# A decode layer on one Trainium2 core: keys, wo and w1 in one transfer each, keys transposed in place, one exp per row

## The chip, the cores and the metric

The kernel runs on one core of one Trainium2 chip. The metric is the device time of one execution in microseconds (us). Before the change it is 139.44 us, the median of three runs (139.34 to 139.45).

The core has five engines with a queue each, which work on their own and wait for each other through semaphores: TensorE (PE; its weight loads are listed as PEld), VectorE (DVE), ScalarE (ACT), GpSimd (POOL) and SyncE (SP), which here only issues transfers. Sixteen DMA engines carry data between the chip's main memory and the on-chip memory of 128 partitions. Matmuls write their sums to PSUM, and another engine has to copy them from there.

## The reference

A transformer layer for one new token in each of four sequences (B = 4, model width D = 1024), in bf16. Everything is read once from main memory; the weights and the cache are nearly all of the data.

```python
def _A_ref(x, k_cache, v_cache, wq, wo):       # 32 query heads, 4 key heads, head width 128
    W = min(4096, max(256, Sk // 4))           # Sk = 8192, so the last W = 2048 positions
    q = (x @ wq).reshape(B, 1, 32, 128).transpose(0, 2, 1, 3)
    k = repeat(k_cache[:, :, Sk - W:, :], 8, axis=1)
    v = repeat(v_cache[:, :, Sk - W:, :], 8, axis=1)
    p = softmax(einsum("bhqd,bhkd->bhqk", q, k) * 128 ** -0.5)
    o = einsum("bhqk,bhkd->bhqd", p, v)
    return o.transpose(0, 2, 1, 3).reshape(B, 1, 4096) @ wo

def _B_ref(x, w1, w3, w2):                     # inner width 3584
    return (silu(x @ w1) * (x @ w3)) @ w2

h  = x + _A_ref(_layernorm(x), k_cache, v_cache, wq, wo)
h2 = h + _B_ref(_layernorm(h), w1, w3, w2)
```

Sizes in bf16: wq 8.4 MB, keys 8.4 MB, values 8.4 MB, wo 8.4 MB, w1, w3 and w2 7.3 MB each.

## The kernel before, in words

**Memory.** All large inputs pass through five slots of 32 KB per partition. `ring` (L106) is the list of what goes through them, in order: the first half of wq (four of its eight rows per partition), the keys of two batches, those of the other two, two slots for transposed keys (which no transfer fills), the second half of wq, the values in two slots, wo in two, w1 in two, w3 in two, w2 in two. `fill` (L118) allocates the next slot and issues its transfers on SP (L132); it goes on until the slot that it wants is the one that was taken five places earlier and is not yet marked as used. `done` (L139) marks a part as used and calls `fill`. The instruction itself waits for the semaphores of the last readers. So each transfer may run up to five slots ahead of its use. Keys, values and wo go as four transfers each of 16 KB per partition, wq as two of 32 KB, w1 and w3 as two of 28 KB each, w2 as six of 14 to 2 KB. SP takes its instructions strictly in order. x itself is small: four transfers of 2 KB on ScalarE's queue (L149).

**Order of the work.** The schedule is written out by hand: each engine takes its instructions in the order of the program.

1. x is loaded, transposed on VectorE (L225) and normalised (`layernorm_T`, L192), with sums over partitions by a matmul (L198).
2. `query(0)` (L237): the first half of x @ wq, 32 matmuls of 512 columns, four at a time on four groups of 32 array columns.
3. Keys (L258 to L270): for each batch and each eight blocks of 128x128, eight transposes on TensorE into PSUM (L264), and one eviction of 1024 columns into a slot of the ring, in turn by VectorE (L266) and ScalarE (L268).
4. `query(1)`, then q is copied (L274, L275), transposed (L278) and spread into `Qm` (L284).
5. Attention, batch by batch and staggered by the loop at L395: `scores` (L295, 16 matmuls of 512 columns per batch, L299), `row_max` (L310), `softmax` (L325), `transpose_p` (L349), `output` (L358). The scores of 8 positions by 4 key heads share a row. `softmax` takes the exponential four times for each batch, once for each key head, with a bias that makes the entries of the other key heads zero (L336 to L339). `transpose_p` turns 32x32 squares on VectorE (L351). `output` sums the row totals by a matmul (L360), multiplies with the values (L374), scales and masks (L383) and folds four parts into one (L391).
6. Attention's output is gathered by eight matmuls (L414), cast, transposed and copied into `oP` (L422 to L427). Then wo: 128 matmuls of 256 columns, four at a time (L439). x is added (L449).
7. The second layer norm, then w1 (gate, L463), exp, plus one, reciprocal (L477 to L481), w3 (up, L463), the product (L485), a transpose (L225), and w2 (L496), which is used in the six pieces in which it comes. The sum with h goes out in four transfers (L510).

## Time and profile before

One execution was profiled. Its own time is 139.33 us and its span, from the first to the last instruction, 137.5 us (137.54 in the trace).

| | before |
|---|---|
| time of the three runs, median | 139.44 us |
| time of the profiled execution | 139.33 us |
| its span | 137.5 us |
| data read | 55.58 MB, 404 GB/s over the span |
| TensorE busy | 78.7 us (57%) |
| VectorE busy | 52.6 us (38%) |
| ScalarE busy | 42.7 us (31%) |
| mean granted clock of TensorE | 0.812 |

How to read it. The page divides the span into 40 slices of 3.44 us, and gives for each engine how much of a slice it was busy, in tenths. The DMA row does this for the mean of the 16 DMA engines. The list of queues says which queue's packets took which share of 16 engines' span; q1 is SP's. The chain of work that ended last is followed back from the end of the program: at each step to what the instruction had waited for. The groups give, for instructions of one line and kind, how often they ran, their total and mean duration, and how long their engine had been idle just before them and for whom. Windows give the busy time of an engine in chosen stretches, with the granted clock of TensorE (1.00 or 0.50 in this trace). The trace also has the records of single instructions, DMA packets and the changes of the clock. A busy share is a mean over stages: the stage tells what a microsecond is worth.

### The profile page before, as it was taken

What the parts mean: (1) busy time and instruction counts of PE and PEld (TensorE: products, weight loads), DVE (VectorE), ACT (ScalarE), POOL (GpSimd) and SP (SyncE); (2) the same over time, 40 slices, a digit from 0 to 9 for tenths busy, and PEclk for the clock granted to TensorE, in tenths of its full rate; (3) what the DMA queues carried; (4) which work ended last, traced back from release to release, by engine and by line L of the source; (5) the groups of instructions that cost most, each with busy time, mean ns of one, the idle gap of its engine ahead of it and who ended that gap; (6) DMA issues with size and microseconds to landing.
All of it is one profiled execution on the core that took longest, in us unless ns stands there. A gap on an engine that the chain in (4) does not pass through costs nothing.

```text
span 137.5 us, 2022 instructions
## 1 busy us (share of the span) xinstructions
PE 78.7 (57%) x866; PEld 45.4 (33%) x868; DVE 52.6 (38%) x97; ACT 42.7 (31%) x57; POOL 4.2 (3%) x18
## 2 busy tenths in 40 slices
PE   0000299999903889328936997948539600834271
PEld 0000139898801422114303353536424300322240
DVE  3001505666700235187165359551330596160001
ACT  1200006989820325998803940000040200000000
POOL 7400000000000000000000000000000000000000
PEclk9999999999995599955595599995995995595555
DMA  5998999999899999999999999999999999999950
GB/s 152 458 459 382 429 434 434 415 438 505 376 410 429 415 438 419 434 429 415 443 417 429 422 467 425 438 417 434 425 430 425 425 447 388 414 437 431 400 219 2
DMA packets 3529, 55.72 MB, mean 405 GB/s; under 512 B 416, under 2 KB 448, under 8 KB 704
## 3 DMA queue, kind: packets, MB, share of 16 engines
q1 hardware_dynamic: 3472, 55.58, 95.2%
q8 instruction: 7, 0.11, 0.3%
q10 hardware_dynamic: 48, 0.01, 0.0%
q14 instruction: 2, 0.02, 0.0%
HBM read 55.58 MB, written 0.01 MB: 404 GB/s over the span
## 4 chain that ended last, share of the span: by engine, by line
DMA 51%; PE 28%; DVE 13%; ACT 4%; issue 2%; SPq 1%; DVEq 0%
DMA s_wq<-in_A_wq_dram 31%; DMA s_w<-in_B_w_dram 20%; PE o_ps L374 11%; ACT P L339 4%; PE y_ps L439 4%; PE sc_ps L299 3%; DVE PT L351 3%; PE q_ps L244 2%; DVE om L391 2%; PE gu_ps L463 2%; DVE od L383 2%; PE tot_ps L360 1%; PE nm_ps L328 1%; PE on_ps L414 1%; SPq L132 1%
## 5 line engine op out<-in xcount | busy, mean ns | idle before, releaser
L339 ACT ACTIVATE P<-sc_ps,bias 128x512 bf16<-128x512 f32 x16 | 19.7, 1421 | 10.8 <-DVE bias L336 10.8
L374 PE MATMUL o_ps<-s_v,PT 128*128 128x512 bf16 x62 | 18.4, 457 | 0.3 <-issue 0.2
L268 ACT COPY s_kT<-kt_ps 128x1024 bf16<-128x1024 bf16 x16 | 15.6, 1012 | 6.8 <-PE kt_ps L264 6.8
L264 PE MATMUL kt_ps<-ident,s_k 128*128 128x128 bf16 x256 | 16.1, 219 | 1.1 <-ACT s_kT L268 1.0
L264 PEld LDWEIGHTS <-s_k 128*128 128x128 bf16 x256 | 15.0, 98 | 2.9 <-issue 2.5
L463 PE MATMUL gu_ps<-s_w,n_T 128*32 128x448 bf16 x128 | 9.8, 474 | 9.8 <-DMA s_w<-in_B_w_dram 8.0
L266 DVE COPY s_kT<-kt_ps 128x1024 bf16<-128x1024 bf16 x16 | 11.1, 692 | 10.1 <-PE kt_ps L264 10.1
L244 PE MATMUL q_ps<-s_wq,n_T 128*32 128x512 bf16 x64 | 7.2, 630 | 7.4 <-DMA s_wq<-in_A_wq_dram 5.6
L496 PE MATMUL y_ps<-s_w,hg_T 128*32 128x256 bf16 x112 | 6.6, 386 | 7.9 <-DMA s_w<-in_B_w_dram 5.3
L374 PEld LDWEIGHTS <-PT 128*128 128x128 bf16 x64 | 7.6, 123 | 9.8 <-issue 5.5
L208 ACT ACTIVATE rstd<-rstd,eps_t 128x4 f32<-128x4 f32 x2 | 0.6, 297 | 32.4 <-DVE rstd L207 32.4
L198 PE MATMUL sums_ps<-both,ones_f 128*128 128x64 f32 x4 | 1.1, 374 | 16.1 <-DVE both L196 16.1
L351 DVE STREAM_TRANSPOSE PT<-P 128x2048 bf16<-128x2048 bf16 x4 | 9.2, 2304 | 2.7 <-ACT P L339 2.7
L463 PEld LDWEIGHTS <-n_T 128*32 128x32 bf16 x128 | 4.4, 122 | 14.5 <-issue 11.5
L299 PE MATMUL sc_ps<-s_kT,Qm 128*32 128x512 bf16 x64 | 8.5, 603 | 0.4 <-DVE Qm L284 0.4
L496 PEld LDWEIGHTS <-hg_T 128*32 128x32 bf16 x112 | 4.2, 124 | 10.8 <-issue 6.8
L383 DVE SCALAR_TENSOR_TENSOR od<-o_ps,rinv,jmask 128x512 f32<-128x512 f32 x4 | 3.0, 750 | 9.4 <-PE o_ps L374 9.3
L198 PEld LDWEIGHTS sums_ps<-both,ones_f 128*128 128x128 f32 x4 | 0.8, 250 | 16.4 <-DVE both L196 16.4
L315 PE MATMUL mx_ps<-ident_f,rmax 128*1 128x128 f32 x8 | 1.9, 333 | 7.4 <-DVE rmax L313 7.4
L244 PEld LDWEIGHTS <-n_T 128*32 128x32 bf16 x64 | 2.4, 139 | 10.8 <-issue 8.6
L479 DVE RECIPROCAL eg<-eg 128x896 f32<-128x896 f32 x1 | 5.8, 5753 | 0.0
L439 PE MATMUL y_ps<-s_wo,oP 128*32 128x256 bf16 x128 | 4.9, 326 | 1.5 <-DVE oP L427 1.5
(68 smaller groups left out, 59.7 us busy)
## 6 DMA issues: line engine op xcount, KB each, us to landing
s_w<-in_B_w_dram SPq DMA_DIRECT2D x4, 3584.0 KB
s_wq<-in_A_wq_dram SPq DMA_DIRECT2D x2, 4096.0 KB, 12.3
s_k<-in_A_k_cache_dram SPq DMA_DIRECT2D x4, 2048.0 KB, 20.5
s_v<-in_A_v_cache_dram SPq DMA_DIRECT2D x4, 2048.0 KB
s_wo<-in_A_wo_dram SPq DMA_DIRECT2D x4, 2048.0 KB, 25.1
s_w<-in_B_w_dram SPq DMA_DIRECT2D x1, 2048.0 KB, 24.7
s_w<-in_B_w_dram SPq DMA_DIRECT2D x1, 1792.0 KB
s_w<-in_B_w_dram SPq DMA_DIRECT2D x1, 1536.0 KB
```

What stands on the lines that cost most here:

```text
L244: nc.tensor.matmul(q_ps[hf][R * c : R * c + R], lhsT=xn_T[:, kc, :], rhs=w[:, kk, o : o + HALF * Dh], start=(kc == 0), stop=(kc == KC - 1) ...
L264: nc.tensor.transpose(out=kt_ps[:, jj], in_=k[:, jb * JB + jj, :], identity=ident[:])
L266: nc.vector.tensor_copy(out=kT[:, jb * JB : (jb + 1) * JB], in_=kt_ps[:])
L268: nc.scalar.copy(out=kT[:, jb * JB : (jb + 1) * JB], in_=kt_ps[:])
L299: nc.tensor.matmul(sc_ps[b][R * q : R * q + R], lhsT=Qm[:, b, g * R : (g + 1) * R], rhs=v[:, g, q], start=(g == 0), stop=(g == Hkv - 1), t ...
L339: nc.scalar.activation(out=P4[:, :, :, g], in_=sc_ps[b][:].rearrange("p (j i) -> p j i", i=L5), func=ACT.Exp, bias=bias[:, g : g + 1], sca ...
L351: nc.vector.transpose(out=PT[:].rearrange("p j h -> p (j h)"), in_=stage.pop(("P4", b))[:].rearrange("p j i g -> p (j i g)"),)
L374: nc.tensor.matmul(o_ps[:], lhsT=PT[:, i * JM : (i + 1) * JM, :].rearrange("p j h -> p (j h)"), rhs=v[:, i * JM : (i + 1) * JM, :], start= ...
L439: nc.tensor.matmul(y_ps[R * c : R * c + R, :], lhsT=oP[:, g, t, :], rhs=w[:, 0, o : o + DQ], start=(g == 0 and t == 0), stop=(g == Hkv - 1 ...
L463: nc.tensor.matmul(out_ps[hf][R * c : R * c + R], lhsT=hn_T[:, kc, :], rhs=w[:, kk, o : o + FH], start=(kc == 0), stop=(kc == KC - 1), til ...
L479: nc.vector.reciprocal(out=eg[:], in_=eg[:])
L496: nc.tensor.matmul(y2_ps[R * c : R * c + R, :], lhsT=hg_T[:, fc, :], rhs=w[:, ff, c * DQ : (c + 1) * DQ], start=(fc == 0), stop=(fc == FC ...
```

## The change

- **Memory.** The five slots become one tile, `ring`, of five units of 32 KB per partition, in which every input has a place written out by hand: wq in units 0 and 1, keys in 3 and 4, values 0 and 1 in 2, values 2 and 3 in 0, wo in 3 and 4, w1 in 1 and 2, w3 in 3 and 4, w2's first piece in 0 and its others in 1. Each transfer waits for the last readers and writers of the bytes that it overwrites, and of no others.
- **Transfers.** The first transfer is one of wq's eight rows (8 KB per partition), the second all keys (64 KB per partition), the third the other seven rows of wq (56 KB). wo goes in one transfer of 64 KB per partition and w1 in one of 56 KB. Values stay at 16 KB per transfer and w3 at 28 KB; w2 goes in pieces of 26, 16, 8, 4 and 2 KB. In all 16 large transfers stand where 24 stood. The transfers are issued from where they stand in the program: values 2 and 3 after half of the query, wo after the last scores, w1 after the matmuls of `output(1)`, w3 and the first piece of w2 after wo's matmuls, the rest of w2 after the gate's.
- **Keys.** A partition now holds 256 positions of one batch and key head. The transposes run in 16 steps of 16 blocks; the evictions write back over the blocks that were read, one of three on VectorE, two on ScalarE. All of them come ahead of the whole query. `scores` reads the transposed keys as pairs of neighbouring elements, 256 bytes apart, instead of single elements 8 bytes apart.
- **Softmax.** The maximum is taken for two batches at once. One exponential per batch goes over the row; VectorE then spreads each value over four columns, times a 0/1 mask of the key head (`spread`), and transposes.
- **After it.** The fold of `output` is two additions on POOL. Attention's output is gathered by four matmuls straight into the layout of `oP`. wo's matmuls are 64 of 512 columns, two at a time, and x is added by four matmuls into the same sum.
- **Layer norm and silu.** The copy and the square run on ScalarE, three small operations on POOL; the plus one of silu runs on ScalarE. Most constants are set up on POOL.

The diff, cut to its core:

```diff
-    wo_v = A_wo.rearrange("(g p t) n -> p g (t n)", g=Hkv, t=T)
+    KI = P // (B * Hkv)
+    KP = W // KI
+    KQ = KI // C
+    k_v = A_k_cache[:, :, Sk - W : Sk, :].rearrange("b g (i j) d -> (b g) i (j d)", j=KP)
+    v_v = A_v_cache[:, :, Sk - W : Sk, :].rearrange("b g (i j) d -> b i g (j d)", j=JR)
+    wo_v = A_wo.rearrange("(p t) n -> p (t n)", t=T)
...
+    ring = stream.tile([P, 5 * UNIT], BF16)
...
+    wq_s = at(0, KC, NQ)
+    k_s = at(3, KP, Dh)
+    v_s = [at((2, 0)[b // 2], 2, JR, Dh)[:, b % 2] for b in range(B)]
+    wo_s = at(3, T, D)
+    w1_s = at(1, KC, F)
+    w3_s = at(3, KC, F)
+    W2B = [13, 8, 4, 2, 1]
...
+    load(wq_s[:, :1, :], wq_v[:, :1, :])
+    load(k_s.rearrange("p j d -> p (j d)"), k_v)
+    load(wq_s[:, 1:, :], wq_v[:, 1:, :])
+    load_values(0)
+    load_values(1)
...
     def layernorm_T(h_T, tag):
-        nc.vector.tensor_copy(out=both[:, 0], in_=h_T[:, :, :B])
-        nc.vector.tensor_tensor(out=both[:, 1], in0=both[:, 0], in1=both[:, 0], op=ALU.mult)
+        nc.scalar.copy(out=both[:, 0], in_=h_T[:, :, :B])
+        nc.scalar.activation(out=both[:, 1], in_=h_T[:, :, :B], func=ACT.Square)
...
+    for n in range(KP // JB):
+        blocks = k_s[:, n * JB : (n + 1) * JB, :]
+        kt_ps = ps.tile([P, JB, P], BF16, tag=("scA", "ktA", "scB")[n % 3])
+        for jj in range(JB):
+            nc.tensor.transpose(out=kt_ps[:, jj], in_=blocks[:, jj, :], identity=ident[:])
+        if n % 3 == 0:
+            nc.vector.tensor_copy(out=blocks, in_=kt_ps[:])
+        else:
+            nc.scalar.copy(out=blocks, in_=kt_ps[:])
...
+    q_ps = ps.tile([P, 2, REP // 2, Dh], FP32, tag="scA")
+    for kc in range(KC):
...
+        if kc == KC // 2 - 1:
+            load_values(2)
+            load_values(3)
...
+    kT = k_s.rearrange("p (u v) (y q l) -> p y q u v l", v=JR, q=C, l=KQ)
...
     def scores(b, gs):
-        v = get("kT", b).rearrange("p j (q i g) -> p g q j i", q=C, g=Hkv)
...
-                    rhs=v[:, g, q],
+                    rhs=kT[:, Hkv * b + g, q],
...
+    def softmax(b):
+        p1 = act.tile([P, W // C], BF16, tag=("hg", "eg")[b % 2], name="p1")
+        nc.scalar.activation(
+            out=p1[:].rearrange("p (v l u) -> p u v l", l=KQ, u=L5 // KQ),
+            in_=sc_ps[b // 2][:, b % 2].rearrange("p (u v l) -> p u v l", l=KQ, v=JR),
+            func=ACT.Exp,
...
+    def spread(b):
+        P4 = ktpool.tile([P, JR * L5, Hkv], BF16, tag="P4")
+        nc.vector.tensor_tensor(
+            out=P4[:],
+            in0=stage.pop(("p1", b))[:].rearrange("p (x o) -> p x o", o=1).to_broadcast([P, JR * L5, Hkv]),
+            in1=gmask[:].to_broadcast([P, JR * L5, Hkv]),
+            op=ALU.mult,
+        )
...
+        o2 = act.tile([P, 2, Dh], FP32, tag="o2", bufs=1)
+        nc.gpsimd.tensor_tensor(out=o2[:], in0=od[:, :2], in1=od[:, 2:], op=ALU.add)
+        nc.gpsimd.tensor_tensor(out=om[:, b], in0=o2[:, 0], in1=o2[:, 1], op=ALU.add)
...
+    scores(0, (0, 1, 2, 3))
+    scores(1, (0, 1, 2, 3))
+    row_max(0)
+    scores(2, (0, 1))
+    bias_of(0)
+    softmax(0)
+    softmax(1)
+    scores(2, (2, 3))
+    scores(3, (0, 1, 2, 3))
+    load(wo_s, wo_v.rearrange("p (t n) -> p t n", t=T))
+    row_max(1)
+    spread(0)
+    bias_of(1)
+    softmax(2)
+    transpose_p(0)
+    spread(1)
+    softmax(3)
+    transpose_p(1)
+    total(0)
+    output(0)
+    spread(2)
+    transpose_p(2)
+    output(1)
+    load(w1_s, w1_v)
+    spread(3)
+    transpose_p(3)
+    total(1)
+    output(2)
+    output(3)
...
+    nc.scalar.copy(out=oP[:, :, :B], in_=on_ps[:].rearrange("p b t -> p t b"))
...
+    for t in range(T):
+        row = wo_s[:, t].rearrange("p (k i n) -> p i k n", k=2, i=2)
+        for i in range(2):
+            nc.tensor.matmul(
+                y_ps[R * i : R * i + R],
+                lhsT=oP[:, t, :],
+                rhs=row[:, i],
...
+    for i in range(2):
+        load(w3_s[:, 4 * i : 4 * i + 4, :], w3_v[:, 4 * i : 4 * i + 4, :])
+    load(w2_s[0], w2_v[:, : W2B[0], :])
...
+    up_projection(w1_s, gate_ps)
+    fc = W2B[0]
+    for w, n in zip(w2_s[1:], W2B[1:]):
+        load(w, w2_v[:, fc : fc + n, :])
+        fc += n
+    nc.scalar.activation(out=eg[:], in_=gate_ps[:, :, :FH], func=ACT.Exp, scale=-1.0)
+    nc.scalar.activation(out=eg[:], in_=eg[:], func=ACT.Identity, bias=1.0)
...
```

`load` issues one transfer on SP, `load_values(b)` the values of batch b, and `at(unit, ...)` is a view of `ring` from a unit on.

## The prediction

> **What bounds the kernel now.** I read three views in this order: the slices and queues of the page, the chain of work that ended last, and the windows of TensorE. The page first:
>
> ```profile
> DMA  5998999999899999999999999999999999999950
> ...
> q1 hardware_dynamic: 3472, 55.58, 95.2%
> ```
>
> The DMA row is at 8 or 9 tenths from the second slice to the thirty-eighth of 40, and SP's queue q1 alone fills 95.2% of the span of all 16 engines. In the trace's DMA packet records the first packet starts at 1.77 us, the last ends at 133.58 us, and in every stretch of 2 us from 2 to 132 the 16 engines are busy for all of it. The chain of waits says the same; columns are start, length, what:
>
> ```profile
> 13.65 29.70 DMA s_wq<-in_A_wq_dram
> ...
> 105.80 27.58 DMA s_w<-in_B_w_dram
> ```
>
> Both are transfers in a queue that never ran dry, and what the chain puts between them (attention, L299 to L427) did not stop the queue. So the kernel costs 55.58 MB at full rate, 1.77 us ahead of it and 3.96 us (137.54 - 133.58) behind it. The profiled execution took 139.33 us, 1.79 more than its span; the three runs have a median of 139.44. There are two ways to change the time: fewer engine-nanoseconds per byte, or a hole in the stream.
>
> **What the larger transfers remove.** Median packet durations in the records: 2 KB 84 ns, 4 KB 159, 8 KB 311, 12 KB 464, 14 KB 538, 16 KB 612, 28 KB 1066, 32 KB 1214. From 16 to 32 KB that is 602 ns per 16 KB and 10 ns fixed. So I estimate 56 KB at 2117 ns, 64 KB at 2418 (at most 2 x 1214 = 2428), 26 KB at 988. Each transfer has 128 packets, 8 per engine. Before, per engine: wq 16 x 1214, K, V and wo 96 x 612, w1 and w3 32 x 1066, w2 8 x (538+464+612+311+159+84), together 129.6 us. After: wq 8 x (311+2117), K 8 x 2418, V 32 x 612, wo 8 x 2418, w1 8 x 2117, w3 16 x 1066, w2 8 x (988+612+311+159+84), together 128.9. The gain is 0.7 us, and 0.05 for eight fewer closing packets of 9 ns. The larger transfers can't give more. Without a hole: 139.33 - 0.75 = 138.6.
>
> **What they add: waits in SP's queue.** SP issues in order. V of batches 2 and 3 lies where wq's rows 0 to 3 were, so it waits for half the query; wo lies on K, so it waits for the last scores. Behind wo stand w1, w3 and w2: a hole ahead of wo moves everything. Before, K was transposed into other slots and SP was far ahead. The stream after, per engine: first load from 1.77, 2.5 us and 0.6 for the slow start (first packets took 1.7 to 2.1 us in place of 1.21), to 4.9; K to 24.2, with x's packets between 24.4; the rest of wq to 41.3; V 0 and 1 to 51.1; V 2 and 3 to 60.9. An issue reaches its first packet in 1.04 us (0.73 to 1.77). So V 2 and 3 must be released by 50.0, and wo by 59.9.
>
> **The chain that releases wo.** All of K must land before a transpose starts: 24.4, 0.4 for the slowest engine, 0.5 to release (the rest of wq ended at 42.9 and PE started at 43.39): 25.3. The rows:
>
> ```profile
> L268 ACT COPY s_kT<-kt_ps 128x1024 bf16<-128x1024 bf16 x16 | 15.6, 1012 | 6.8 <-PE kt_ps L264 6.8
> L264 PE MATMUL kt_ps<-ident,s_k 128*128 128x128 bf16 x256 | 16.1, 219 | 1.1 <-ACT s_kT L268 1.0
> ...
> L266 DVE COPY s_kT<-kt_ps 128x1024 bf16<-128x1024 bf16 x16 | 11.1, 692 | 10.1 <-PE kt_ps L264 10.1
> ```
>
> Until K is there the engines have only the first layer norm, part of which moves to ScalarE and POOL: it took 3.6 us (13.35 to 16.95) and has until 25, as x now follows a first load of 2.5 us instead of 9.7. Sixteen evictions of 2048 columns replace 32 of 1024; ScalarE makes ten. No row has that width; L275 (512 columns) took 586 ns, so 426 ns per 512, and 2048 take 1.86 us, 1.84 start to start (two of 1012 run in 1.95). The bounds are 1.7 and 2 x 1.012. VectorE's take 1.25 (692 to 1384). Two steps of 16 transposes at the half clock (107 ns each, 128 columns at 1.2 GHz) come first: 28.7. ScalarE then bounds it; its eighth eviction, at 43.4, frees the buffer of step 14. Two steps at 62 ns (32 in 2.0 us) end at 45.4, and VectorE's copy at 46.7. Query: 16 groups of four at 0.22 us (at full clock the w1 groups of 448 columns run 0.19 apart) give 3.5 us and 0.2 to drain, 50.5. Half of it is done at 48.7, so V 2 and 3 go out in time. ScalarE's copy of q (1024 columns, 1.0), eight transposes (0.7) and the copy into Qm (0.3) make 52.6. Scores of batches 0 and 1: 8 groups x 0.23 and 0.2, 54.6. The maximum over 1024 columns (690 ns for 512, so 1.22), mx (0.42), the second maximum over 512 (278 ns for 128, so 0.68), nm (0.4): 57.4. Six more groups, 1.6: **the last scores end near 59.0**, 0.9 ahead of the limit. Two things in this can go wrong.
>
> The clock:
>
> ```profile
> 17.43:20.85 3.42, 3.42 (x36) 1.00 1.01 431
> 20.85:24.26 3.41, 3.25 (x56) 1.00 1.01 432
> 34.50:37.91 3.41, 3.13 (x52) 1.00 0.97 408
> 37.91:41.33 3.42, 0.00 (x0) 1.00 0.88 378
> 41.33:44.74 3.41, 1.35 (x16) 0.50 1.01 432
> ...
> 54.98:58.39 3.41, 1.31 (x11) 1.00 1.03 437
> 58.39:61.81 3.42, 0.63 (x9) 0.50 1.01 431
> ```
>
> Columns: stretch, length, PE busy, granted clock, DMA. The clock changes at steps of 3.41 us: in the same view stretches with up to 1.58 us of work ended the full clock, one with 2.22 did not. Nothing but transposes ran from 20.5 to 37.7 and it stayed full, so transposes count; I take it that they also raise it, which no row shows, because the query always ran ahead of them. [...]
>
> The scores' rate:
>
> ```profile
> 52.86 1.03 PE L299 MATMUL sc_ps<-s_kT,Qm 128*32 128x512 bf16 x8
> ...
> 108.30 1.70 PE L463 MATMUL gu_ps<-s_w,n_T 128*32 128x448 bf16 x32 [1.19 <-DMA s_w<-in_B_w_dram]
> ```
>
> Two groups of scores take 1.03 us at the full clock, 0.43 apart, where eight groups of w1 take 1.70, 0.19 apart. The scores read every fourth key element (8 bytes apart); w1 is read contiguously. After the change scores read two neighbours and then go 256 bytes on. The bounds are 0.22 (contiguous) and 0.43 (single elements); I take 0.23, as pairs make one 4-byte read for two elements. [...]
>
> **Further down.** After the last scores at S, VectorE has 1.9 us of maxima, then four spreads and four transposes. A spread (2048 outputs) isn't in the trace: between 1.25 (a copy) and 2.30 (L351, as wide); I take 2.3. Output 1 ends near S + 17, and w1 must be released by S + 20 (59.9 + 19.3 - 59.0): covered, and if the clock is low it ends at S + 19, still covered. Output 3's od ends near S + 29, POOL's two adds 1.0 (128 columns took 0.29; 0.9 to 1.8, where L391 took 1.05), on_ps 1.1, the copy 0.3, so wo's matmuls start at S + 31.4. They are now pairs of 512 columns: twice the column time. w3's first half needs 14 of 32 rows: 14 x 0.22 to 0.43, so S + 34.5 to 37.5, and its release is due at S + 37 (wo 19.3, w1 16.9 behind 60.9). Covered by about 1 us; if S is late both shift together. What the change takes off ScalarE (twelve of the 16 exps, 1.42 us each) and puts on it (parts of the layer norm, the +1 of silu) is on no path that stops the stream; nor are the four matmuls that add x into wo's sum, which run while oP is copied. If that cover were gone they would cost 4 x 0.11. The second layer norm, the gate and the 5.75 us reciprocal (L479) end ahead of w2's last rows, as now; the table load now between gate and exp (1.28 us) is hidden behind w3. The tail after the last packet is unchanged.
>
> **Rivals.** (1) The scores stay at 0.43: 14 groups x 0.2 = 2.8 us, S = 61.8, a hole of 1.9, and 140.5; with one low-clock stretch more, 142. For it: the new stride is longer; against it: pairs. This one ends slower than before, and decides once S passes 60.5. (2) The clock falls in one of the pauses (45.4 to 46.7, 50.5 to 52.6, 54.6 to 57), or x lands late behind 64 KB packets (eight small packets alternate with 2.4 us ones) and holds up the layer norm, whose matmul stands ahead of the transposes: 1.3 to 1.7 us on S, a hole of 0.4 to 0.8, 139.0 to 139.5. (3) Transposes never raise the clock: 256 x 107 ns = 27.4 from 25.3, query from 54, half at 57.4, V 2 and 3 7.4 us late; S near 68.3, wo another 0.9 late: 147, or 150 with rival 1. (4) The changed transfers do nothing for the rate, because 64 KB packets run as four of 16 KB: 139.2 and no hole; small, and inside (2).
>
> **Numbers.** Forecast, no hole or one under 0.3 us: 138.7, chance 0.50 (faster 0.41, same 0.08, slower 0.01). Rivals 2 and 4: 0.16 (same 0.05, slower 0.11). Rival 1: 0.25, slower. Rival 3: 0.09, slower. Within 0.2% (139.16 to 139.72) is about what a measurement can't tell from no change. Faster 0.41, same 0.13, slower 0.46. The range reaches from 138.3 (a start of the stream without its 0.6 us counts half) to 142.3 and leaves out rival 3 and little else; that of the forecast alone is 138.3 to 139.2. Both signs hold much, because S stands 0.9 us from its limit.
>
> **What would show it.** The DMA row stays at 9 through the slices near 61 us (44% of the span) if I am right; a low slice there, and wo's SP wait for sc_ps behind V's landing, is rival 1 or 3. PEclk while transposes run decides 3; the time from group to group on the scores' line decides 1; idle time of L225's transposes for the first-sum matmul decides 2. If the stream has no hole and the time is not near 138.7, my packet arithmetic is wrong.

## The result, and the profile after

The changed kernel takes 169.03 us (median of six runs, 167.38 to 170.67) where the kernel before takes 139.33 beside it: a ratio of 1.209, with a 95% interval of 1.204 to 1.215 (one run, 170.67, is left out of the ratio as disturbed). The forecast was 138.7, and its range ended at 142.3. The profiled execution took 169.39 us, its span is 167.18.

The slices and the queue of the changed kernel, one slice being 4.18 us:

```profile
DMA  5999993999599979999607988999997999999960
GB/s 214 289 251 251 236 220 63 236 251 251 192 425 439 425 321 400 412 435 435 290 0 251 502 376 376 502 439 439 439 429 336 432 436 425 412 420 417 410 244 3
...
q1 hardware_dynamic: 2320, 55.58, 91.0%
```

Two things are to be seen. In the first 11 slices the DMA row is full but for two dips (a slice holds less than one round of 5 us packets; in the packet records hardly any engine is idle there), yet the rate below it is mostly 190 to 290 GB/s where it is mostly over 400 later: the engines are busy for the whole time and carry about half as much. And the twenty-first slice is empty: 0 in both rows. The queue's share fell only from 95.2 to 91.0%, in a span 30 us longer; read alone, it would say that the stream still binds as it did.

The chain of waits of the changed kernel (start, length, what):

```profile
1.19 46.36 DMA ring<-in_A_k_cache_dram
47.60 3.61 PE kt_ps L225 x32
51.23 14.26 ACT ring L229 x8
65.54 1.96 PE kt_ps L225 x32
67.52 1.24 DVE ring L227
68.80 3.66 PE q_ps L238 x64
72.48 1.02 ACT q_sb L250
...
74.62 6.13 PE sc_psscA L279 x20
...
84.32 4.47 PE sc_psscB L279 x15
...
134.22 28.79 DMA ring<-in_B_w_dram
```

The last key packet ends at 46.42, where the forecast had 24.8, and the first transpose starts at 47.60 (forecast 25.3). From there to the first score the steps take what was worked out for them; the scores do not. SP's waits name what the empty slice waited for:

```profile
SPq L125 <- PE sc_psscB L279: 17.4, 1, 17.4
```

In the packet records the last packet of the values ends at 83.79, wo is issued at 88.85 when the last scores have been read, and its first packet starts at 89.81. Over the 22 us around it the 16 engines are idle for 7.4 us on the mean.

The packet durations (medians, ns) say where the first half went:

```
                        64 KB keys   64 KB wo   56 KB wq   56 KB w1   16 KB values
forecast                   2418        2418       2117       2117         612
changed kernel             5126        2420       2120       2116         614
(mean)                     5033        2495       2205       2121         618
```

The estimate holds to 0.2% for three of the four large transfers, by the medians. The keys' packets, as long as wo's and written to the same units 3 and 4, take twice that.

### The profile page after: what moved, and what is told of

Its sections match the earlier page's. It is cut to its first block, busy times and chain, and to the rows that moved or that the text cites. A ratio compares the mean times of both kernels' runs of the same rounds, so it can differ in the third digit from the quotient of the medians.

```text
span 167.2 us, 1796 instructions
## 1 busy us (share of the span) xinstructions
PE 77.3 (46%) x788; PEld 44.8 (27%) x788; DVE 46.7 (28%) x43; ACT 36.4 (22%) x33; POOL 15.0 (9%) x39
## 4 chain that ended last, share of the span: by engine, by line
DMA 45%; PE 27%; DVE 13%; ACT 10%; issue 2%; POOL 1%; SPq 0%; POOLq 0%; DVEq 0%; ACTq 0%
DMA ring<-in_A_k_cache_dram 28%; DMA ring<-in_B_w_dram 17%; ACT ring L229 9%; PE o_ps L366 5%; PE y_ps L445 4%; DVE P L333 4%; PE sc_psscB L279 4%; PE sc_psscA L279 4%; PE kt_ps L225 3%; DVE PT L355 3%; PE q_ps L238 2%; PE gate L470 2%; DVE rmax L291 1%; DVE od L374 1%; DVE ring L227 1%
## 5 line engine op out<-in xcount | busy, mean ns | idle before, releaser
L225 PE MATMUL kt_ps<-ident,ring 128*128 128x128 bf16 x256 | 17.1, 234 | 11.0 <-DMA ring<-in_A_k_cache_dram 8.3
L229 ACT COPY ring<-kt_ps 128x2048 bf16<-128x2048 bf16 x10 | 17.8, 1915 | 10.8 <-PE kt_ps L225 10.8
L225 PEld LDWEIGHTS <-ring 128*128 128x128 bf16 x256 | 16.5, 106 | 11.7 <-DMA ring<-in_A_k_cache_dram 8.5
L366 PE MATMUL o_ps<-ring,PT 128*128 128x512 bf16 x64 | 16.2, 416 | 5.0 <-DVE PT L355 3.5
L227 DVE COPY ring<-kt_ps 128x2048 bf16<-128x2048 bf16 x6 | 7.3, 1225 | 20.4 <-PE kt_ps L225 20.4
L383 POOL TENSOR_TENSOR o<-od 128x256 f32<-128x256 f32 x4 | 6.8, 1695 | 66.8 <-DVE od L374 66.8
L507 PE MATMUL y_ps<-ring,hg_T 128*32 128x256 bf16 x112 | 6.1, 374 | 8.5 <-DMA ring<-in_B_w_dram 8.5
L333 DVE TENSOR_TENSOR P<-p,gmask 128x2048 bf16<-128x2048 bf16 x4 | 9.1, 2269 | 0.0
L445 PE MATMUL y_ps<-ring,oP 128*32 128x512 bf16 x64 | 7.1, 379 | 0.1
L279 PE MATMUL sc_psscB<-ring,Qm 128*32 128x512 bf16 x32 | 6.5, 866 | 0.0
L279 PE MATMUL sc_psscA<-ring,Qm 128*32 128x512 bf16 x32 | 6.1, 859 | 0.5 <-DVE Qm L260 0.5
```

Of the source, the lines that this page charges most:

```text
L225: nc.tensor.transpose(out=kt_ps[:, jj], in_=blocks[:, jj, :], identity=ident[:])
L227: nc.vector.tensor_copy(out=blocks, in_=kt_ps[:])
L229: nc.scalar.copy(out=blocks, in_=kt_ps[:])
L279: nc.tensor.matmul(sc_ps[b // 2][R * q : R * q + R, b % 2], lhsT=Qm[:, b, g * R : (g + 1) * R], rhs=kT[:, Hkv * b + g, q], start=(g == 0), ...
L333: nc.vector.tensor_tensor(out=P4[:], in0=stage.pop(("p1", b))[:].rearrange("p (x o) -> p x o", o=1).to_broadcast([P, JR * L5, Hkv]), in1=g ...
L366: nc.tensor.matmul(o_ps[:], lhsT=PT[:, i * JM : (i + 1) * JM, :].rearrange("p j h -> p (j h)"), rhs=v_s[b][:, i * JM : (i + 1) * JM, :], s ...
```

## The experiments

Theory A at the start: two separate costs, the key load (how, was open) and the slow reads of the scores, which leave wo late. Rivals: the long rows as such (theory B in the first expectations); the place of the key load, beside x's small transfers (theory C); the distance of the key heads in main memory (theory A's own guess at how); a third cost that these two hide. All kernels below are the changed one with the edit shown. Medians are quoted with the kernel before run beside them where there were several rounds; the others are one execution.

### The old key layout and reads, all else changed

```diff
-    k_v = ...rearrange("b g (i j) d -> (b g) i (j d)", j=KP)
+    k_v = ...rearrange("b g (i j) d -> b i g (j d)", j=JR)     # four transfers of 16 KB, 32x4 rows each
-    kT = k_s.rearrange("p (u v) (y q l) -> p y q u v l", v=JR, q=C, l=KQ)
+    kT = k_s.rearrange("p (b j) (q i g) -> p b g q j i", b=B, q=C, g=Hkv)
-            out=p1[:].rearrange("p (v l u) -> p u v l", l=KQ, u=L5 // KQ),     # in softmax, as the scores' order
+            out=p1[:],                                                         # changes with the layout
```

> Only the layout of the keys goes back to that of before: four transfers of 16 KB per partition, partition = (position block, key head) of one batch, so that neighbouring rows lie 16 KB to 2 MiB apart in turn and the 16 engines work on rows 32 KB apart; scores read every fourth element (8 bytes apart). All else is as changed. Theory A (the changed key transfer is slow because its 16 engines walk rows exactly 2 MiB apart in step): 16 KB key packets at 612 ns, keys landed by 25.5 us; scores 0.43 us from group to group, last scores near 60, no hole of more than 0.5 us, 138.6 to 139.5 us. Theory B (rows of 64 KB from the cache are slow, whatever their addresses): the same here. Theory C (the second transfer of the program is slow, whatever it reads, because x's small transfers run beside it): key packets near 1.28 us, keys landed at 46, 158 to 162 us.

Measured: 140.48 us, 1.0091 of before (1.0057 to 1.0125). Key packets 611 ns, keys done at 25.9; 32 score matmuls in 3.62 us, which is the old 0.43 a group. So 28.5 of the 29.7 us come with the key layout, its reads and the order in which the exp writes (0.69 us for one exp here; 1.40 to 3.75 in the changed kernel). The key load stands at the same place, beside x's transfers, and is fast: theory C falls. The DMA row has no hole:

```profile
DMA  4999999996989999997999998998899999999920
```

but wo was issued at 59.47, first packets began at 60.83 and took up to 3339 ns.

### The new layout in four transfers of 16 KB

```diff
-    load(k_s.rearrange("p j d -> p (j d)"), k_v)
+    for n in range(4):      # a quarter of each row
+        load(part_n_of(k_s), k_v[:, :, n * KP // 4 * Dh : (n + 1) * KP // 4 * Dh])
```

> The keys keep the changed layout, so engines still work on rows 2 MiB apart, but come in four transfers of 16 KB per partition. Theory A: 16 KB packets at 1.28 us (a quarter of the 5.13 us that 64 KB took), last keys at 46 us, transposes done by 54, query at 64 when wq has landed, last scores near 84, a hole of 1 to 2 us: about 164 us. Theory B (long rows): packets at 612 ns, last keys at 25, query at 42 to 49, last scores near 65 with the slow scores, a hole near 5 us: 143 to 145 us. Theory C: as A.

Measured: 164.75 us; packets of 16 KB took 1268 to 1282 ns (medians of the four transfers), still half the rate. The length of the rows is not the cause: theory B falls.

### Key heads not 2 MB apart, with the changed and with contiguous reads

```diff
+    # rows of 64 KB, 8 of every 31, so that the groups stand 1.94 MB apart
+    k_v = A_k_cache.rearrange("b g (i j) d -> (b g i) (j d)", j=KP)[: 16 * 31].rearrange("(y z) n -> y z n", z=31)[:, :KI]
# second kernel, besides:
-                    rhs=kT[:, Hkv * b + g, q],
+                    rhs=k_s[:, 4 * (16 * b + 4 * g + q) : 4 * (16 * b + 4 * g + q) + 4, :],
```

> The keys come in one transfer of 64 KB per partition as changed, but of other rows: 16 groups of eight rows that lie 31 x 64 KB = 1.94 MiB apart in the cache in place of 32 x 64 KB = 2 MiB (so it scores the wrong positions; all work is done). Theory A: packets at 2.42 to 2.50 us, keys landed near 25.6, last scores 41.2 us later as in the changed kernel (67), wo's first packet at 68 where V ends at 61: a hole of 7 us and 145 to 147 us. Theories B and C: packets at 5.0 us, 167 to 171 us as changed.

> As e3, and the scores read four whole transposed blocks (512 contiguous elements) in place of pairs 256 bytes apart, so that the scores are of wrong columns; number and size of the matmuls are unchanged. If the pairs' stride is what makes a group of scores take 0.75 us: groups 0.22 us apart, last scores near 59 to 60.5, no hole over 0.6 us, and the forecast's own 138.6 to 139.3 us comes out once both mis-sized terms are taken away (theory A for the keys). If something else slows the scores: 0.75 stays and 145 to 147 us as in e3. With theory B or C for the keys: about 161 us.

Measured: 168.56 and 160.76 us. The packets stayed at 5119 and 5104 ns, so the exact power of two is not the cause: theory A's guess falls. The contiguous reads settle the other half. The DMA row of the second kernel, from its page:

```profile
DMA  5999669990979998999999897999989999999960
```

and its scores among the groups (its L281 is the changed kernel's L279):

```profile
L281 PE MATMUL sc_psscA<-ring,Qm 128*32 128x512 bf16 x32 | 1.9, 380 | 0.5 <-DVE Qm L262 0.5
```

Eight groups took 1.91 us, 0.22 apart, where the changed kernel's page has

```profile
L279 PE MATMUL sc_psscA<-ring,Qm 128*32 128x512 bf16 x32 | 6.1, 859 | 0.5 <-DVE Qm L260 0.5
```

6.09 us, 0.76 apart. No slice after the tenth is empty (the 0 there is a dip between rounds of the long key packets): the last scores end at 80, ahead of the last value packet at 83.9. wo is issued at 80.00, 2.1 us before its first packet, and its first-round packets take 2492 at most.

### The key load and the reads by themselves

Two kernels that only load and read. Each transfer has its own row length, so that the packet records tell them apart.

```diff
+    load(24, rows(k16, 32)) ... load(18, rows(k16, 128))        # 16 groups of 8 rows, 0.5 to 2 MB apart
+    every_8_bytes = a[:, :2048].rearrange("p (n s) -> p n s", s=4)[:, :, 0]     # 24 matmuls of 512 columns for each step
```

> No layer is computed: nine transfers of 128 rows, then matmuls on what they brought, and zeros go out. Each transfer has 16 groups of eight rows, 64 KB from row to row, and a row length of its own, by which its packets are told apart; the groups lie 0.5 MiB apart (24 KB rows), 0.56 (23), 1 (22), 1 MiB + 16 KB (21), 1.5 (20), 1.94 (19) and 2 MiB (18), 2 MiB in the values' cache (17). Theory A2 (each engine takes eight rows that follow each other, and the 16 are slow when they read from places far apart): full rate, 26.8 GB/s per engine (a 24 KB packet 0.91 us), at 0.5 and 0.56 MiB, and near 12.8 at 1.94 and 2 MiB in both caches (an 18 KB packet 1.44 us); where it turns is open. Theory A1 (a distance that is a power of two) fell with the rows 1.94 MiB apart, unless 1 MiB is slow and 1 MiB + 16 KB is not. Last, 16 KB rows in another order: 16 rows 64 KB apart as the outer dimension, eight groups 2 MiB apart as the inner. If engines take rows that follow each other, all 16 are in one 1 MiB stretch at a time: 0.61 us; if rows are dealt out in turn: about 1.28. Matmuls at the full clock, four at a time, from group to group: contiguous 0.22 us, the order of before 0.43, the changed one (pairs 256 bytes apart) 0.75. If cost goes by the number of new 16-byte lines, single elements every 16, 32 and 256 bytes cost the same, and pairs half of that. If the distance counts by itself, 256 bytes cost more than 32.

Measured: 16 groups of 8 rows took twice the full-rate time at every distance from 0.56 to 2 MB (23 KB 1823 ns, 20 KB 1576, 18 KB 1416), and on the other cache too (17 KB 1337); only the first, whose 128 rows lie in one run of equal steps and so are one dimension, ran at the full rate (24 KB 919). Distance fell; the form of the transfer remained.

> A kernel that only loads and reads; its output is zeros, it computes nothing of the reference. Nine loads from the key cache, told apart by row length, and reads by TensorE at growing steps. Theory A3 (form: an outer dimension of 16 gives each engine eight neighbouring partitions, and in step they meet on the same ways into SBUF; 32 or more outer entries do not): 16x8 rows hardly off a single run (24 KB, groups 528 KB apart) half rate, 1840 ns; 32x4 near (22 KB, 256 KB apart) 843 and 32x4 far (20 KB, 1 MB apart) 767 ns, 64x2 far (18 KB) 690, one dimension of 128 rows 256 KB apart (23 KB) 881: all full rate; 8x16 (15 KB) half or worse, 1150 or more; the same 16 outer x 8 as before, 16 KB, 1254. On 64 partitions alone: 16x4 (14 KB) and one dimension of 64 (13 KB) both half, 1074 and 996, since the partitions and not the form would count. Rival A2b (distance, once a row is not a single run): the far ones 1534 and 1380, the near ones full. Rival A4 (the form alone, partitions without part in it): 13 KB at full rate, 498. Reads, 24 matmuls: 1.5 us contiguous, every 4 B 1.6, 8 B 2.9, 16 B 5.6, 32 B 5.7; if only 16-byte lines count, 64, 128 and 256 B at 5.7 too; if distance adds, between 5.7 and 10.4 for 64 and 128.

Measured, in ns (the full rate is 38.3 ns per KB, from the 919):

```
form, distance                       row     measured   full rate
16 of 8, 528 KB apart               24 KB      1911         919
32 of 4, 256 KB apart               22 KB       841         843
32 of 4, 1 MB apart                 20 KB       764         766
64 of 2, 512 KB apart               18 KB       686         689
one dimension, 256 KB apart         23 KB       874         881
16 of 8, outer 64 KB, inner 2 MB    16 KB      1254         613   (from the first of the two kernels)
8 of 16, 4 MB apart                 15 KB      1848         575   (beside another transfer)
```

So 32 or more outer entries run at the full rate at the distances tried, and 16 entries of 8 do not. This kernel's two transfers into 64 partitions (13 KB 1132, 14 KB 1015) ran beside others, as did its repeat of the 16 KB form (1674), and decide nothing. What this leaves open is whether the half rate arises on the way into on-chip memory or in the form. In the next kernel each transfer waits for the one before:

```diff
+    load(P // 2, 22, one[: P // 2])        # the full-rate form, into 64 partitions only
+    nc.sync.dma_start(out=far[...], in_=rows[..., : 13 * 512])      # the slow form, into main memory
```

> A kernel that only loads; its output is zeros, it computes nothing of the reference. One transfer at a time, each waiting for the one before, told apart by row length; at the full rate a packet takes 918 ns for 24 KB and in proportion. Theory A3p (the half rate arises where the packets go: in step, engines meet on the same ways into SBUF): 128 rows of one dimension (24 KB) 918; 16x8 rows 2 MB apart (23 KB) 1760; one dimension of 64 partitions (22 KB) 1680 though its form is that of the full-rate transfer; 16x4 rows on 64 partitions (21 KB) 1610; one dimension of 32 partitions (20 KB) 1530 and of 16 (19 KB) 1450 or twice that; 8x16 (15 KB) 1150 or more; and the 16x8 rows copied to DRAM instead of SBUF (13 KB) at the same rate as 128 rows of one dimension copied there (12 KB), whatever that rate is. Theory A4 (the half rate comes from the form or from the reading side, eight rows one behind the other in each engine): one dimension of 64, 32 and 16 at the full rate (841, 764, 726), 16x4 on 64 partitions slow, and to DRAM the 16x8 rows take about twice what the 12 KB rows take in proportion.

```
                                         row     measured   full rate
one dimension, 128 partitions           24 KB       912        919
16 of 8, 128 partitions                 23 KB      1818        881
one dimension, 64 partitions            22 KB      1755        843
16 of 4, 64 partitions                  21 KB      1624        804
one dimension, 32 / 16 partitions      20/19 KB  1431/1747   766/728
8 of 16, 128 partitions (8 engines)     15 KB      1122        575
16 of 8 into main memory                13 KB       506        498
one dimension into main memory          12 KB       464        460
```

The transfers' issues of this kernel, with KB in all and us from issue to landing, show the first two:

```profile
buf<-in_A_k_cache_dram SPq DMA_DIRECT2D x1, 3072.0 KB, 9.7
buf<-in_A_k_cache_dram SPq DMA_DIRECT2D x1, 2944.0 KB, 17.2
```

The slow form is not slow into main memory (506 ns, full rate 498), and the fast form is slow into 64 partitions (1755, full rate 843): the half rate arises where packets are written. Into 64 and 32 partitions a packet takes 1.9 to 2.1 times the full-rate time, into 16 partitions 2.4 times (1747 against 728; one packet per engine). How the written side halves the rate, no run shows: that engines in step meet on the same ways into on-chip memory, as theories A3 and A3p have it, is a guess. Which engine took which rows and wrote which partitions no record shows, nor why 32 outer entries of 4 run at the full rate (22 KB in 841 ns, full rate 843) where 16 of 8 do not (24 KB in 1911, full rate 919).

### Keys from one run of 8 MB, without and with contiguous reads

```diff
-    k_v = A_k_cache[:, :, Sk - W : Sk, :].rearrange("b g (i j) d -> (b g) i (j d)", j=KP)
+    k_v = A_k_cache.rearrange("b g (i j) d -> (b g i) (j d)", j=KP)[:P]      # one dimension of 128
# second kernel: the contiguous rhs as above
```

> The changed kernel with its 128 rows of 64 KB taken from one run of 8 MB of the key cache, so that the load is one dimension of 128; the keys are those of other positions than the reference's, sizes and all else are the same. Theory A (form of the key load, plus the slow reads of the scores): key packets 2420 ns instead of 5033, keys landed near 25.5; the last score matmul as long after that as in the changed kernel (41.2 us), 66.7; V's packets done near 61, so a hole of some 6 us before wo as in the changed kernel; time 145 (144 to 147). Rival B1 (64 KB packets to these units are slow by themselves once they are the first big transfer, or x's packets between them cost): packets stay above 4000, time over 160. Rival B2 (the hole belongs to the late keys, not to the scores): no hole, 139.

> The same as the kernel with the rows in one run, and the score matmuls read their 512 columns contiguously (the scores are then of other keys, in another order; sizes and counts are the same). Both costs that the forecast missed are then away, and the rest of the change stays. Theory A: key packets 2420 ns, scores 0.22 us a group, last score near 58 to 59 (32.4 us after the keys, as in the run with far rows and contiguous reads), no hole above 1 us before wo; time 138.5 to 139.6, the forecast's own number less what its gain by larger transfers was too large. Rival C (the change has a third cost that the two hid: exp spread by VectorE, the shared VectorE and GpSimd work, w3 released late): 140.5 or more with no hole before wo.

Measured: 146.81 us, 1.0527 (1.0509 to 1.0546), and 140.09 us, 1.0051 (1.0019 to 1.0084), with single runs from 139.3 to 141.11. Key packets 2418 ns, landed at 24.6. The first kernel's DMA row, from its page:

```profile
DMA  4996969969969999808696969969999999999940
```

and SP's wait for the scores:

```profile
SPq L125 <- PE sc_psscB L279: 17.2, 1, 17.2
```

The hole is there, at the eighteenth slice, with the keys on time (wo issued at 65.68, the engines idle for 5.8 us on the mean). So theory A's two costs separate:

| | groups of 8 rows | one run |
|---|---|---|
| scores in pairs | 169.03 | 146.81 |
| scores contiguous | 160.76 (one execution, groups 1.94 MB apart) | 140.09 |

The form of the key load costs 22.2 or 20.7 us, the reads 8.3 or 6.7 (7.8 between the two single executions with groups 1.94 MB apart). But 140.09 is above what was expected, and the runs spread over 1.8 us: something more than the two costs is left, as rival C had it, though less than it gave. Its profile has no hole, yet wo, issued at 59.05, began at 60.56 with first packets of up to 3965 ns instead of 2418, and the engines' last packets ended as late as 134.85, though near 132.7 on the mean.

### The query ahead of the keys, with large and with small transfers

```diff
-    load(keys); load(wq_s[:, 1:, :], ...)
+    load(wq_s[:, 1:, :], ...); load(keys)        # old key layout; the query's matmuls ahead of the transposes
# second kernel, besides: wo in four transfers of 16 KB, w1 in two of 28 KB
```

> The kernel with the old key layout in four transfers (e1), and in addition all of wq is loaded ahead of the keys and the query, its copy and transposes come ahead of the key transposes. wo and w1 still go in one transfer each. The last scores should end near 56 us in place of 59.4, so wo is released 4 us before V's last packet and the stream has no hole and no slow restart (in e1 the first round of wo's packets took up to 3.3 us). If e1's 1.2 us over before is that hole and restart: 139.2 to 139.9. If it is the uneven finish of the engines that 64 KB and 56 KB packets bring: 139.9 to 140.6, with the slowest engine still 1.9 us behind the mean at the end.

> e5 with wo in four transfers of 16 KB per partition and w1 in two of 28 KB, as before. If packet length made the difference to before: 138.9 to 139.4 and the slowest engine about 1.2 us behind the mean at the end. If not: as e5.

Measured: 139.30 us, 1.0008 (0.9991 to 1.0025), and 139.45, 1.001 (1.0002 to 1.0019). wo was issued at 58.75, 0.7 earlier than with the old layout alone, and none of its packets passed 2514 ns. So the 1.2 us of the old-layout kernel go when the late start goes, as the first expectation's first case had it, and the length of wo's and w1's packets makes no difference that the time shows. The queue's packet time per engine fell to 130.47 from before's 130.97 with the large transfers, to 130.85 with the small ones; the time did not fall.

### wo in two halves

```diff
     scores(1, (0, 1, 2, 3))
+    load(wo_s[:, : T // 2, :], ...)        # over the keys of batches 0 and 1, which are then read
...
-    load(wo_s, wo_v.rearrange("p (t n) -> p t n", t=T))
+    load(wo_s[:, T // 2 :, :], ...)
```

> The kernel with the old key layout (140.48 before this), and wo loaded in two halves of 32 KB per partition, the first issued once the scores of the first two batches have read their keys, the second after the last score as before. In the run with the old key layout wo was issued at 59.47 and began at 60.83, and the first two packets of most engines took up to 3339 ns instead of 2420; where wo was issued at 58.75 (query ahead of the keys) none was above 2514 and the time was 139.30. Theory D (a transfer issued when the queue has nearly run dry starts slowly, and spreads the engines' ends; this is the rest of the old-layout kernel's 1.2 us): with the first half issued near 56 its packets take 1213 and none above 1700, time 139.2 to 139.6. Rival E (the 1.2 us come from elsewhere, the softmax with VectorE's spread or w3's release): the slow packets go and the time stays 140.2 to 140.8.

> The kernel with the key rows in one run and contiguous reads (140.09, 139.3 to 141.11; keys of other positions, read in another order), with wo in the same two halves. There wo was issued at 59.05, began at 60.56, and its first packets took up to 3965 ns. Theory D: no first packet above 1700, the spread of the times closes, 139.2 to 139.6, which is before's time, so that all of the change but its key load and its score reads is worth nothing measurable. Rival E: the time stays near 140.1 with its wide spread. Third case, the larger transfers do pay once nothing is late: 138.6 to 139.0.

Measured: with the old layout 139.53 us, 1.0016 (1.0004 to 1.0028), after 140.48 without the halves: 0.95 us less, clear of the spread of the runs. With one run and contiguous reads 139.52, 1.0022 (1.0005 to 1.004), after 140.09: 0.6 less, but the two intervals overlap, and the times still spread over 1.2 us (139.18 to 140.37), which theory D had expected to close. The first halves were issued at 54.1 and 54.2, and no packet of wo was above 1224 ns. So theory D holds for the packets in both kernels, and for the time in the old layout: a transfer issued 1.4 to 1.5 us before its first packet, with the queue nearly empty, began with slow packets, which cost 0.5 (old layout) and 0.9 us per engine in all, though no slice is empty. Issued 2.1 us before (the query ahead of the keys; contiguous reads with late keys) it did not, and there wo's packets were of 64 KB, so it is not the halves' shorter packets that help. The DMA rows of the second kernel without and with the halves, where wo starts in the eighteenth slice:

```profile
DMA  4996969897979999997999999999899999999920
```

```profile
DMA  4997978996979999999999999989999998999930
```

The eighteenth and nineteenth digits are 9 and 7 without the halves, 9 and 9 with them; but digits of 6 to 8 stand wherever long packets run, so the row alone does not tell. The loss stands in the durations of some 20 of wo's 128 packets, not in idle time.

### One early key transfer or four

```diff
# the last kernel (keys from one run, contiguous reads, wo in halves), with the keys in quarters of a row
```

> The kernel with key rows in one run, contiguous score reads and wo in halves (139.52; keys of other positions, read in another order), with the keys in four transfers of 16 KB per partition instead of one of 64. In every execution of the five kernels that load the keys in one transfer the time is 2.16 to 2.29 us more than the span; in the six with the keys in four transfers 1.59 to 1.71; before 1.79. Theory F (this goes with the single early key transfer, and took most of what the larger transfers gained): span 137.2 to 137.7, time less span 1.65, time 138.9 to 139.3, so faster than the kernel with one transfer although its packets are four times smaller. Rival G (the extra comes from something else, the layout of the rows or the reads): time less span stays at 2.2, and the time at 139.5 or, with 8 x 10 ns x 3 more of fixed cost per packet, 139.7.

Measured: 139.39 us, 1.0001 (0.9992 to 1.001). The time less the span was 1.62 to 1.71 in all 11 executions, where it is 2.17 to 2.29 with one transfer: theory F's first half holds. Its second does not: the median span rose from 137.3 to 137.7, so the time stayed. What did close is the spread: 139.13 to 139.55, in place of 139.18 to 140.37. Packet time per engine is 130.53 and 130.36, before 130.97.

## Why the prediction was wrong, point by point

**"What bounds the kernel now": right.** Without the two costs and the late start of wo, every version lies at 139.3 to 139.5, with its DMA row full to the end.

**The larger transfers, "64 KB at 2418": this step failed, in the term K 8 x 2418.** It took 8 x 5033: 20.9 us more. The length of a packet was scaled rightly; that all transfers of 128 packets write at the same rate was assumed without a word. The runs showed that a transfer of 16 outer entries of 8 rows goes into on-chip memory at half the rate, whatever the length of the rows (medians of 1268 to 1282 ns for 16 KB, 5126 for 64 KB) and the distance of the groups that was tried. No row of before had 16 outer entries: wq, wo, w1 had one dimension, keys and values 32 of 4. Rival 4 asked whether long packets gain anything, which is another question; no rival had a transfer slower than the nearest row.

**The gain of 0.75: there in the stream, a little smaller, and not in the time.** Packet time per engine fell by 0.4 to 0.6 where wo was not late. With one key transfer the span's median was 137.3 against before's 137.5; then the 2.2 us outside the span, instead of 1.79, took it back. The forecast's 138.7 was thus out of reach by 0.6 to 0.8 us with everything else as forecast.

**"The stream after": wq's other seven rows and wo took 0.7 and 0.6 more** (means of 2205 and 2495 ns), most of it in first packets after a change or a stop.

**The chain that releases wo: right up to the scores.** From keys landed to the last eviction 21.2 us (forecast 21.4), query 3.66 (3.7), from the query's start to Qm ready 5.8 (5.9). The group rows:

```profile
L225 PE MATMUL kt_ps<-ident,ring 128*128 128x128 bf16 x256 | 17.1, 234 | 11.0 <-DMA ring<-in_A_k_cache_dram 8.3
L229 ACT COPY ring<-kt_ps 128x2048 bf16<-128x2048 bf16 x10 | 17.8, 1915 | 10.8 <-PE kt_ps L225 10.8
...
L227 DVE COPY ring<-kt_ps 128x2048 bf16<-128x2048 bf16 x6 | 7.3, 1225 | 20.4 <-PE kt_ps L225 20.4
```

ScalarE's 2048 columns: 1915 (1860 forecast); VectorE's 1225 (1250).

**The clock: right.** Between keys and query nothing but transposes ran, and in the chain above the first 32 take 3.61 us and a later 32 take 1.96: transposes raised the clock (granted in full from 51.9; from start to start 0.107 us before that, 0.056 after). The forecast's 107 ns at the half clock is the rate in the trace of before: at a granted 0.50 q's eight transposes (L278, from 47.44) start 0.107 us apart, and the query's groups of 512 columns (L244, from 43.80) 0.427, which is 1.2 columns per ns. Rival 3 fell.

**The scores' rate, "bounds 0.22 and 0.43; I take 0.23": this step failed too.** It was 0.76. The upper bound was the rate of single elements 8 bytes apart; pairs 256 bytes apart looked gentler, with a pair reckoned as one read; single reads stand in no record. TensorE's reads at growing steps, 24 matmuls each (six groups), from the timeline of the second of the kernels that only load and read (start, us):

```profile
92.78 1.46 PE L122 MATMUL acc<-buf 128*32 128x512 bf16 x24
94.07 1.54 PE L125 MATMUL acc<-buf 128*32 128x512 bf16 x24
95.43 2.94 PE L128 MATMUL acc<-buf 128*32 128x512 bf16 x24
98.16 5.61 PE L131 MATMUL acc<-buf 128*32 128x512 bf16 x24
103.56 5.72 PE L134 MATMUL acc<-buf 128*32 128x512 bf16 x24
109.07 5.83 PE L137 MATMUL acc<-buf 128*32 128x512 bf16 x24
114.70 8.44 PE L140 MATMUL acc<-buf 128*32 128x512 bf16 x24
122.87 12.22 PE L143 MATMUL acc<-buf 128*32 128x512 bf16 x24
```

The steps are contiguous, then 4, 8, 16, 32, 64, 128 and 256 bytes; starts are 0.22, 0.22, 0.45, 0.90, 0.92, 0.94, 1.36 and 1.8 us apart per group. So up to 4 bytes apart is free, 8 bytes double the time, 16 to 64 bytes make it four times as long, and beyond 64 bytes distance costs by itself. Pairs 256 bytes apart take half the time of the last row, 0.9, in the same kernel, and 0.76 in the changed one. Four neighbours per 256 bytes take 0.53, eight 0.26. The lines of 16 bytes of the expectations stand in no record; what shows is that two elements in every 16 bytes (the step of 8) give 0.45, four (the step of 4) 0.22, and that steps of 16 to 64 bytes cost nearly alike.

**Rival 1 had the right place and sign, not the size.** It said that wo would wait once S passed 60.5; with the keys on time S was 65.6 and the time 146.81, where rival 1 gave 140.5 to 142.

**"0.9 ahead of the limit", no hole, no cost: wrong.** With S at 59.0 and contiguous reads there was no hole, as forecast, and wo's first packets still took up to 3965 ns; in the time this is some 0.6 us, within the spread of those runs, and 0.95 us in the old layout, where wo was issued at 59.47. The limit was reckoned from the first packet; by the packets, issuing at 58.75 was early enough and 59.05 was not.

**Further down: right in order.** From S = 88.8: w1 issued at S + 14.3 (output 1 was to end at S + 17), spreads 2.27 us each (2.3), wo's matmuls from S + 30.6 (31.4), w3 released at S + 33.8 (34.5 to 37.5), tail 3.96 as before. POOL's last two adds 0.73 and 0.47 (1.0).

**The sum.** Forecast span 136.9, keys 20.9, hole 7.4, wq and wo 1.3: 166.5 of 167.18. The other 0.7, as near as the packet records tell: the slowest engine ended some 1.8 us after the mean one, before some 1.0.

## What to carry to other kernels

A transfer's rate can belong to its form as well as to its packet size: before merging transfers, count the outermost dimension on the reading side (16 entries of 8 rows took 1911 ns for 24 KB, 32 of 4 took 841 for 22 KB), and take the price of a form that no row shows from a load that does nothing else. The row of one stride for TensorE's operand gives no upper bound for another (0.43 us a group at 8 bytes, 0.76 for pairs 256 bytes apart): it takes a read of its own at that stride, or an eviction that writes in an order that makes the read contiguous (not tried here). Where a load must wait for the last reader of its place, split it so that the part that comes free first keeps the queue fed: here the larger transfers saved 0.4 to 0.6 us of packet time per engine, and one late issue cost up to 0.95 us.

## What the runs showed of the hardware that was not expected

- One transfer of 128 rows as 16 groups of 8 ran at 13.0 GB/s per engine into on-chip memory (64 KB in 5033 ns) where one dimension, or 32 of 4, ran at 27 (24 KB in 919 ns, 22 KB in 841); into main memory 16 groups of 8 and one dimension ran alike (13 KB in 506 ns, 12 KB in 464).
- x's small packets, eight on each of four engines behind slow 64 KB packets, were done at 36.4 us in place of 12.5 (at 19.6 with fast keys in 64 KB packets, 8.8 with fast keys by 16 KB). The wait for the keys covered it.
- While the pair reads ran, ScalarE's exp of 512 columns slowed as well. The changed kernel's timeline, TensorE and then ScalarE:

```profile
84.25 4.52 PE L279 MATMUL sc_psscB<-ring,Qm 128*32 128x512 bf16 x24
```

```profile
84.55 3.75 ACT L320 ACTIVATE p<-sc_psscA,bias 128x512 bf16<-128x512 f32 x1 [9.75 <-DVE bias L314]
```

It took 1.42 us with contiguous reads beside it, where nothing else had changed, and 1.40 with no scores beside it. Why, no run shows. Apart from this, the order in which the exp writes counts: in the kernels with the old key layout it writes its row in order and took 0.69 us, with the old reads beside it.
- POOL's first add took 2.6 to 2.7 us while VectorE spread a row, 0.73 alone; the four make 6.8 us, where the forecast allowed 0.9 to 1.8 for both adds of a batch. It lay on no path that ended late.
- The time beyond the span is 2.16 to 2.29 us in all 35 executions of the kernels with the keys in one transfer and 1.59 to 1.71 in all 50 with four, 1.74 to 1.92 before. What happens there no record shows.
- The row of granted clocks says nothing ahead of its first record: it shows full clock from the start, while the first 32 transposes ran at half the later rate (0.107 us from start to start, later 0.056).
